# Attention tiles of batches 2, 4 and 6: matmuls in two 64-row halves of the array instead of four 64 x 64 quarters

## The chip, the cores and the metric

The kernel runs on one core of one Trainium2 chip. The metric is the device time of one execution in microseconds (us); of several runs the median is given. The profiled execution is one further run, with a span (first to last instruction) of its own and a time of its own.

## The reference

Linear attention without a softmax, normalised per head, is followed by an MLP mixer over tokens and channels. All data are float32.

```python
kv  = einsum('bhsd,bhse->bhde', k, v)        # 64 x 64 for each of 8 batches and 8 heads
out = einsum('bhsd,bhde->bhse', q, kv)       # 576 rows each: the part that the change touches
out = out / sqrt(mean(out*out, -1) + 1e-6) * g_norm
x   = out.transpose(0, 2, 1, 3).reshape(8, 576, 512)
h   = relu(x.transpose(0, 2, 1) @ w_tok1) @ w_tok2     # tokens: 576 -> 256 -> 576
u   = x + h.transpose(0, 2, 1)
y   = u + relu(u @ w_ch1) @ w_ch2                      # channels: 512 -> 1536 -> 512
```

## The kernel before

Batches are worked in four pairs (0 to 3). Each pair goes through attention, then token mixing; after the last pair the channel mixing follows, with two levels of a Strassen-like scheme (products `ps_a`, `ps_b`, `ps_d`, `ps_v`, `ps_w`, `ps_c`), and takes most of the time. While pair n is in token mixing, the attention of pair n+1 is woven into it. That order is written out by hand in lists of short names (`start`, `middle`, `steady`, `last`, L1391 to L1458) that `play` calls one after the other; `keep` holds each engine to this program order.

The names that matter here: `kv..` and `kr.` form k'v of a batch (`kv`, L399, and `kv_rem`, L417); `e..` copies it to `kvp[side]`, where the rows 0 to 63 hold the even head and the rows 64 to 127 the odd head of each of four head pairs (`hp`). `a0` to `a3` are `attend(c)` (L465): c = 0 and 1 are the first batch of the pair (side 0), c = 2 and 3 the second batch; each makes 256 rows of the attention output for all 8 heads. `a4` (`attend_rem`) makes the last 64 rows of both batches. `q..`, `g..` and `t..` read the result from PSUM (square on ScalarE; product with the gain and sum on VectorE). `h..` and `hr` are the first token product (`tok1`; `tok1_rem`, L621), `u0` to `u8` the second (`tok2`). Pair 0 uses other functions (`attend_tile`), so `attend` serves pairs 1, 2 and 3.

In TensorE's program order the tiles c = 0 and 1 stand so:

- pair 1: `hr`, **a0**, `u0 u1 u2`, **a1**, `kv10`
- pairs 2 and 3: `h00 h01`, **a0**, `h10 h11`, `hr`, **a1**, `kv10`

Each matmul of `attend` contracts over the 64 entries of a head: the stationary operand (`lhsT`) is a slice of q with 64 columns, which are rows of the output, and the moving operand (`rhs`) is a 64 x 64 block of `kvp`. The rows of the array follow from the head (h), the columns from the output's partitions (n), so four matmuls (n, h) stand in four quarters of the array. The two heads write to two PSUM tiles, `o[0]` and `o[1]`. There are 2 t x 4 hp x 2 n x 2 h = 32 matmuls in a call. In the profile each float32 matmul appears as two passes (two LDWEIGHTS and two MATMUL records), 64 for a call. `tok1_rem` also contracts over 64 rows, a batch in each half of the rows, with 128 stationary columns and 512 moving ones. All these matmuls go through the helper in L136 and have this line in the profile; they are told apart by their tiles and their array forms, written as rows*columns (64*64, 64*128, 128*128).

Of the kernel before, what the change touches and what calls it, by code (L numbers as in the profile page):

```python
# [20 lines left out]
def kernel(  # L21
# [33 lines left out]
    P = 128  # L55
# [5 lines left out]
    J, JJ, HF, Q = 4, 5, 64, 32  # L61
# [73 lines left out]
    def matmul(*a, **kw):  # L135
        keep(nc.tensor.matmul(*a, **kw))  # L136


    qT, q_rest = {}, {}
# [249 lines left out]
    def attention(pair, groups):  # L389
# [75 lines left out]
        def attend(c):  # L465
            n = "o" if c else "kv"
            o = [ps[n].tile([P, 2, HP, D], F32, name="ps_o", tag=n) for _ in range(2)]
            side = c // 2
            for t in range(2):
                for hp in range(HP):  # L470
                    for n in range(2):
                        for h in range(2):
                            r = ds(h * D, D)
                            matmul(o[h][ds(n * HF, HF), t, hp],
                                   lhsT=qT[2 * pair + side][r, hp, ds((2 * (c % 2) + t) * P + n * HF, HF)],
                                   rhs=kvp[side][r, hp, :D], start=True, stop=True)
            for h in range(2):
                bank[c, h] = o[h].rearrange("p t k d -> p (t k) d")
# [113 lines left out]
        for c in range(5):  # L592
            if whole:
                steps |= {f"a{c}{t}": do(attend_tile, c, t) if c < 4 else attend_tile_rem
                          for t in range(parts(c))}
            else:
                steps[f"a{c}"] = do(attend, c) if c < 4 else attend_rem
            for h in range(parts(c)):
                steps |= {f"{n}{c}{h}": do(f, c, h) for n, f in zip("gqt", (gain, square, total))}
            for t in range(1 if c == 4 else 2):  # L600
                steps |= {f"{n}{c}{t}": do(f, c, t) for n, f in zip("spd", (scale, scale_pool, scale_vector))}
# [957 lines left out]
```

## Time and profile before

| | |
|---|---|
| time, median of 3 runs | 768.65 us (768.58 to 768.66) |
| profiled execution | 768.43 us |
| its span | 766.6 us |
| PE (TensorE matmul) busy | 761.2 us, 99% of the span |
| PEld (weight load) busy | 613.0 us, 80% |
| VectorE, ScalarE, GpSimd busy | 644.5, 279.0, 110.8 us |
| granted TensorE clock | 1.000 |
| `ps_o` passes in quarters (64*64) | 768 (12 calls of `attend`), PE busy 13.8 us |

"PE busy" joins the spans of overlapping passes; what a pass costs in a dense stretch is read from the distance between the starts of two stretches in the timeline. A pass's own duration also holds its way through the array, which overlaps with the next ones. The last matmul ends 3.2 us before the span does.

### The profile page before, as it was taken

How to read it: one execution, taken by the hardware profiler on the slowest of the kernel's cores; microseconds unless marked ns; L12 is line 12 of the kernel's file. 1: busy time of each engine (PE TensorE's matmuls, PEld its weight loads, DVE VectorE, ACT ScalarE, POOL GpSimd, SP SyncE). 2: the span in 40 equal slices, each digit the busy share in tenths (PEclk: the TensorE clock that was granted, in tenths of full speed). 3: DMA queues.
4: the chain of work that ended last, by engine and by line, in shares of the span. 5: the costliest groups of instructions: out<-in, count | busy, mean ns of one | idle time of the engine just before them, and what ended most of it. 6: DMA issues, size and time to landing. Idle time of an engine off the chain costs nothing.

```text
span 766.6 us, 12767 instructions
## 1 busy us (share of the span) xinstructions
PE 761.2 (99%) x4694; PEld 613.0 (80%) x4694; DVE 644.5 (84%) x958; ACT 279.0 (36%) x563; POOL 110.8 (14%) x121
## 2 busy tenths in 40 slices
PE   9999999999999999999999999999999999999998
PEld 8655555446888888888888888888888888888887
DVE  3868896997757779899969889997898996798997
ACT  3656575773210232511234242123352223325211
POOL 0003030203410000002240002042000218000204
PEclk9999999999999999999999999999999999999999
DMA  9999999799799785589998578999649879845689
GB/s 353 325 331 375 318 380 329 252 319 350 252 289 321 288 283 170 175 270 216 216 231 246 157 214 227 261 187 264 202 145 293 166 225 205 209 147 152 153 203 121
DMA packets 138941, 188.28 MB, mean 246 GB/s; under 512 B 48896, under 2 KB 97536, under 8 KB 136832
## 3 DMA queue, kind: packets, MB, share of 16 engines
q1 hardware_dynamic: 103200, 168.72, 69.1%
q0 software_dynamic: 34848, 18.36, 16.0%
q8 instruction: 38, 0.62, 0.3%
q10 hardware_dynamic: 832, 0.39, 0.2%
q14 instruction: 23, 0.19, 0.1%
HBM read 138.28 MB, written 49.15 MB: 244 GB/s over the span
## 4 chain that ended last, share of the span: by engine, by line
PE 96%; DMA 2%; DVE 1%; SPq 0%; ACT 0%; issue 0%; DVEq 0%
PE ps_d L136 28%; PE ps_b L136 19%; PE ps_a L136 19%; PE ps_u L136 8%; PE ps_h L136 8%; PE ps_v L136 5%; PE ps_c L136 3%; PE ps_w L136 2%; PE ps_kv L136 2%; PE ps_o L136 2%; DMA raw<-in_moe_w_tok_dram 2%; DMA v_in<-in_v_dram 1%; PE ps_r L136 0%; DVE x L506 0%; DVE ms L534 0%; DVE w_tok L213 0%
## 5 line engine op out<-in xcount | busy, mean ns | idle before, releaser
L136 PE MATMUL ps_d<-ui,w 128*128 128x256 f32 x504 | 118.6, 379 | 0.0
L136 PEld LDWEIGHTS ps_d<-ui,w 128*128 128x128 f32 x504 | 95.8, 190 | 13.0
L133 ACT COPY ps_d<-ps_a 128x768 f32<-128x768 f32 (+1 forms) x56 | 32.0, 572 | 199.9 <-PE ps_a L136 196.9
L127 DVE TENSOR_TENSOR v<-v,v 128x1536 f32<-128x1536 f32 (+2 forms) x70 | 103.3, 1483 | 0.3
L136 PE MATMUL ps_b<-sv,w 128*128 128x256 f32 x324 | 78.9, 379 | 0.0
L136 PE MATMUL ps_a<-v,w 128*128 128x256 f32 x324 | 78.7, 379 | 0.0
L1288 POOL DMA_DIRECT2D out_dram<-us x24 | 26.8, 1836 | 291.8 <-ACT p L133 286.5
L136 PEld LDWEIGHTS ps_b<-sv,w 128*128 128x128 f32 x324 | 61.2, 190 | 8.9 <-issue 0.6
L136 PEld LDWEIGHTS ps_a<-v,w 128*128 128x128 f32 x324 | 61.6, 190 | 8.4
L136 PE MATMUL ps_u<-h,w_tok 128*128 128x512 f32 (+1 forms) x160 | 64.7, 599 | 0.0
L130 ACT ACTIVATE v<-v 128x768 f32<-128x768 f32 (+1 forms) x54 | 42.7, 822 | 55.1 <-DVE v L127 50.7
L136 PE MATMUL ps_d<-v,w 128*128 128x256 f32 x258 | 62.7, 379 | 0.0
L136 PE MATMUL ps_h<-x,w_tok 128*128 128x512 f32 x128 | 57.6, 600 | 0.7 <-DVE w_tok L213 0.6
L1288 POOL DMA_DIRECT2D out_dram<-r x40 | 41.3, 1926 | 102.0 <-ACT p L133 80.3
L136 PE MATMUL ps_d<-sv,w 128*128 128x256 f32 x228 | 55.4, 379 | 0.0
L136 PEld LDWEIGHTS ps_d<-v,w 128*128 128x128 f32 x258 | 49.0, 190 | 6.6
L136 PEld LDWEIGHTS ps_u<-h,w_tok 128*128 128x128 f32 (+1 forms) x160 | 25.6, 179 | 31.1 <-issue 27.0
L136 PEld LDWEIGHTS ps_d<-sv,w 128*128 128x128 f32 x228 | 43.3, 190 | 5.9
L136 PE MATMUL ps_a<-uT,w 128*128 128x256 f32 x192 | 46.7, 379 | 0.0
L136 PEld LDWEIGHTS ps_h<-x,w_tok 128*128 128x128 f32 x128 | 23.5, 190 | 28.3 <-issue 24.2
L136 PE MATMUL ps_b<-ui,w 128*128 128x256 f32 x168 | 40.8, 379 | 0.0
L136 PEld LDWEIGHTS ps_a<-uT,w 128*128 128x128 f32 x192 | 36.5, 190 | 5.0
(176 smaller groups left out, 1294.7 us busy)
## 6 DMA issues: line engine op xcount, KB each, us to landing
w<-parts SPq DMA_DIRECT2D x168, 384.0 KB
w<-parts SPq DMA_DIRECT2D x56, 192.0 KB
uT<-blocks SPq DMA_DIRECT2D x36, 256.0 KB
k_in<-in_k_dram SPq DMA_DIRECT2D x8, 1024.0 KB
v_in<-in_v_dram SPq DMA_DIRECT2D x8, 1024.0 KB
qT<-in_q_dram SPq DMA_DIRECT2D x8, 1024.0 KB
out_dram<-x POOLq DMA_DIRECT2D x16, 512.0 KB, 6.8
raw<-in_moe_w_ch_dram SPq DMA_DIRECT2D x8, 768.0 KB
```

The source lines that it names most:

```text
L127: keep(engine.tensor_tensor(out=o, in0=a, in1=b, op=op))
L130: keep(nc.scalar.activation(o, a, AF.Relu))
L133: keep(nc.scalar.copy(o, a))
L136: keep(nc.tensor.matmul(*a, **kw))
L1288: keep(nc.gpsimd.dma_start(to, t()[ds(b * Q, Q), at].rearrange("p n l j -> p n (l j)"), accum_op=ALU.add))
```

## The change

For c = 0 and 1 the two matmuls of a head pair and row block that differ only in their 64 columns become one with all 128 columns. The output partitions of this one matmul are 0 to 127; the array rows are still those of the head. A call then has 16 matmuls of the form 64*128 (32 passes) in place of 32 of the form 64*64. The tiles c = 2 and 3 and `attend_rem` stay in quarters. No other instruction on any engine changes place, operands or waits. Six calls are touched: a0 and a1 of pairs 1, 2 and 3.

```diff
             side = c // 2
+            wide = P if c < 2 else HF
             for t in range(2):
                 for hp in range(HP):
-                    for n in range(2):
+                    for n in range(P // wide):
                         for h in range(2):
                             r = ds(h * D, D)
-                            matmul(o[h][ds(n * HF, HF), t, hp],
-                                   lhsT=qT[2 * pair + side][r, hp, ds((2 * (c % 2) + t) * P + n * HF, HF)],
+                            matmul(o[h][ds(n * wide, wide), t, hp],
+                                   lhsT=qT[2 * pair + side][r, hp, ds((2 * (c % 2) + t) * P + n * wide, wide)],
                                    rhs=kvp[side][r, hp, :D], start=True, stop=True)
```

## The prediction

> **What bounds the kernel now.** I read the page first. Its engine line and its chain of work that ended last:
>
> ```profile
> PE 761.2 (99%) x4694; PEld 613.0 (80%) x4694; DVE 644.5 (84%) x958; ACT 279.0 (36%) x563; POOL 110.8 (14%) x121
> ...
> PE 96%; DMA 2%; DVE 1%; SPq 0%; ACT 0%; issue 0%; DVEq 0%
> ```
>
> TensorE works all the time and the chain runs through it. The reader should then ask whether it ever waits for anybody. The list of waits of PE, complete, answers:
>
> ```profile
> PE ps_j L136 <- DVE ones L1366: 1.1, 1, 1.1
> PE ps_h L136 <- DVE w_tok L213: 0.6, 1, 0.6
> PE ps_kv L136 <- DMA v_in<-in_v_dram: 0.4, 1, 0.4
> ```
>
> Three waits, and the last of them ends at 28.0 us (the `ps_h` one). From there to the end of its last matmul PE has no idle time; after that comes a tail of 3.2 us for the output. The first touched call starts at 44.4 us. So what a touched call takes more or less on TensorE moves everything behind it by the same amount: no wait lies behind it that could swallow a delay or eat up a gain. The question is only how long 16 matmuls in halves take against 32 in quarters. That is read from the timeline of PE (start, length, count); a stretch's cost is the distance to the next start:
>
> ```profile
> 110.12 0.46 PE L136 MATMUL ps_kv<-v_in,k_in 64*64 64x64 f32 x16
> 110.40 1.11 PE L136 MATMUL ps_o<-kvp,qT 64*64 64x64 f32 x64
> 111.44 7.13 PE L136 MATMUL ps_h<-x,w_tok 128*128 128x512 f32 x16
> 118.51 1.16 PE L136 MATMUL ps_o<-kvp,qT 64*64 64x64 f32 x64
> 119.60 7.13 PE L136 MATMUL ps_h<-x,w_tok 128*128 128x512 f32 x16
> 126.67 1.99 PE L136 MATMUL ps_h<-x,w_tok1r 64*128 64x512 f32 x8
> 128.58 1.16 PE L136 MATMUL ps_o<-kvp,qT 64*64 64x64 f32 x64
> 129.67 2.48 PE L136 MATMUL ps_kv<-v_in,k_in 128*64 128x64 f32 x80
> ```
>
> 118.51 is a0 and 128.58 is a1 of pair 3: 1.09 us each, for 64 passes, that is 16 rounds of four quarters. The six touched calls hold 6 x 1.09 = 6.5 us, 0.85% of the time. This is all that the change can touch.
>
> **What a round costs.** Each pass needs its stationary operand loaded. The groups of weight loads, forms kept apart (busy us, mean ns):
>
> ```profile
> L136 PEld LDWEIGHTS ps_o<-kvp,qT 64*64 64x64 f32 x768 | 12.3, 135 | 7.6 <-issue 5.3 <-PE ps_h L136 1.5 <-ACT h L130 0.8
> L136 PEld LDWEIGHTS ps_o<-kvp,qT 128*128 128x128 f32 x64 | 7.5, 192 | 0.6 <-issue 0.5
> L136 PEld LDWEIGHTS ps_h<-x,w_tok1r 64*128 64x128 f32 x32 | 2.8, 186 | 4.2 <-issue 4.2
> ```
>
> A load of 128 columns takes 51 to 57 ns longer than one of 64, whether it has 64 rows or 128: columns cost, rows don't. The change halves the number of loads and doubles the columns of each. How closely loads follow each other is seen in narrow windows of the weight loads' timeline: first the remainder product `ps_h<-x,w_tok1r`, the only work before that uses the array in the form that the change chooses, then the quarters of a1:
>
> ```profile
> 126.66 0.19 PEld L136 LDWEIGHTS ps_h<-x,w_tok1r 64*128 64x128 f32 x2 [0.76 <-issue]
> ...
> 126.77 0.19 PEld L136 LDWEIGHTS ps_h<-x,w_tok1r 64*128 64x128 f32 x2
> ...
> 128.58 0.15 PEld L136 LDWEIGHTS ps_o<-kvp,qT 64*64 64x64 f32 x4 [0.76 <-PE ps_h L136]
> ...
> 128.64 0.27 PEld L136 LDWEIGHTS ps_o<-kvp,qT 64*64 64x64 f32 x12
> ```
>
> In the halves two loads run together, one for each half (x2, both done in 0.19), and the next two start 0.11 us later. In the quarters four run together and the next four start 0.055 us later. So loads of different parts of the array overlap, and a part takes its next weights every 0.11 us with 128 columns, every 0.055 with 64.
>
> The moving operand stays 64 wide. A 512-wide pass takes 0.429 us (16 passes 7.07 us, and 32 passes 13.93 us elsewhere in the timeline; the difference by 16), so 64 columns take about 0.053. In quarters load and pass are even, and the round is (1.09 less 0.15 at the ends) / 16 = 0.058. In halves the load is twice as long as the pass and sets the round. The nearest dense row of 128-column loads is pair 0's extra tile:
>
> ```profile
> 14.19 1.06 PE L136 MATMUL ps_og<-kvg,qT 128*128 128x128 f32 x8
> 15.08 1.95 PE L136 MATMUL ps_o<-kvp,qT 128*128 128x128 f32 x16
> ```
>
> 8 passes in 0.89 us, 0.111 each. Its pass is as long as its load, so it bounds a round of halves from above, if the halves overlap; the bare distance of loads, 0.109, bounds it from below. I take 0.111, since it holds the hand-over from load to pass that the quarters show too (0.058 against 0.055).
>
> The Trainium skill, "TensorE: Matmul & The Clock Gate", section "LDWEIGHTS (loading the stationary operand)", says that a load takes its columns divided by 1.2 in ns, whatever its rows, 107 ns for 128: a rule that speaks against this change. By it alone the sum below would be 4.0 us instead of 4.5; the trace's 0.109 to 0.111 is a little above, and I use the trace.
>
> **The ends of a stretch.** 16 passes of 128x512 take 7.07 us where 16 x 0.429 is 6.86: 0.21 us goes at the ends when the array form changes. One part is the load with nothing beside it, 0.11 (the quarters' call 110.40, which follows quarters, takes 1.04 and not 1.09: 0.05, one 64-column load). The rest, 0.10, is the emptying of the array: `ps_kv` at 110.12, with quarters behind it, goes over to them without it (0.28 us for four rounds of 0.058 and a load), while 1.09 - 16 x 0.058 - 0.055 leaves 0.10 for calls with another form behind. The wait of PE for itself shown at 128.58 is this: the record of the pass before it ends later than that start, so no wait for a result is in it.
>
> **The sum.** A call in halves between other forms: 16 rounds x 0.111 = 1.78, plus a first load of 0.11, plus emptying 0.10, less 0.058 since behind the last pass no load is awaited: 1.93 us, 0.84 more than 1.09. This holds for a1 of pair 1 and a0 of pairs 2 and 3: 3 x 0.84 = 2.52.
>
> The other three (a0 of pair 1, a1 of pairs 2 and 3) stand right behind `hr`, which has the form 64*128 already. For them the change takes away one change of form: 0.09 of emptying behind `hr` (0.52 from its last pass to the next start, of which the pass is 0.43), and the first load goes under `hr`'s last pass, 0.11. Its operands are there: `kvp` is copied for a0 of pair 1 by 43.0 us, over 0.8 us before. So 0.84 - 0.20 = 0.64 each, 3 x 0.64 = 1.92. On their other side, and between all other stretches, the changes of form stay as they are.
>
> Sum: +4.5 us. On the profiled execution's 768.43 that makes 772.9; the median of the runs stands 0.22 above it, so 768.65 + 4.5 = 773.1, slower by 0.58%.
>
> Everything else I cost at nothing. ScalarE and VectorE read the same PSUM tiles with the same instructions, 0.6 to 0.8 us later; next to use these banks are `kv10` or the next pair of calls, which stand behind on TensorE and move with it. DMA loads get 4.5 us more, and PE waits for none of them. If this cover failed, the eviction of one tile (0.68 us) would show as a wait of `ps_kv`; I see no reason.
>
> Bounds: the round 0.109 to 0.115 (the upper is an estimate: the hand-over of 0.003 that the quarters show, doubled and rounded up), times 16 x 6: -0.2 to +0.4. The gain behind `hr` 0 to 0.6. Together +4.3 to +5.5, or 773.0 to 774.2. The low end goes to 772.4, since distances are read to 0.01 us and several make up a call, some 0.1 a call. The far rows, 0.058 and 0.22 a round, are the rivals that follow.
>
> **Rivals.**
>
> *The moving operand still sets the round.* If a half took its 128 columns as two sets of 64 side by side, as the quarters do, a round would stay 0.058: 16 of them as now, and only the gain behind `hr` is left, 3 x (0.09 + 0.05) = 0.4 us. Time 768.2, no change. It decides if loads follow at less than 0.06. For it: the quarters do fill the whole array in 0.055. Against it: the 0.11 between loads in the very same form. Chance 0.06.
>
> *Passes bound by their number.* The quarters start a pass every 0.94 / 64 = 0.015 us. If that were the limit, 32 passes would take 0.48: 6 x 0.46 = 2.8 us less, with the gain behind `hr` 3.2, 765.4. Against it: `ps_kv` in two column halves (129.67, 80 passes in 2.41) starts one every 0.030, so the limit is per part of the array, not per instruction; and 16 passes of 0.053 in one half can't be done in 0.48. Chance 0.02. The same skill page, in "Wait — 56ns, not 53.3ns?", gives a floor of about 25 ns from start to start however small the matmul; by it the quarters would take 1.6 and the halves 0.8 us a call, 4.8 us saved. The trace disagrees with 15 ns.
>
> *Halves don't overlap when loads are dense.* In `hr` a load has 0.43 us of pass to hide under; in the new calls it has 0.053. If the two halves took turns, a round would be 0.22: 16 x 0.11 x 6 = 10.5 us on top, 783.6. If a load only couldn't run under its own half's pass, 0.165 a round, 778.3. Against: quarters load and pass at the same rate without either. Chance 0.03 for both.
>
> *It isn't what it says:* the instructions listed for the changed kernel are 128x64, 16 in a call, in six calls, with the same waits, so 0.01.
>
> **How the numbers follow.** The forecast has 0.88. A difference within 0.2% (1.5 us) is about what a measurement of this kernel can't tell from none; the first rival lies there, with most of the last: 0.07. Faster: 0.02. Slower: 0.91. The forecast's own range, 772.4 to 774.2, holds the 8 in 10 and needs no other case.
>
> **What would show it.** In the profile after: 192 `ps_o` passes of form 64*128, 64x64 moving, with 384 left in quarters; the distance from such a call to the next start 1.93 us between other forms and about 1.83 behind `hr`, with `hr` itself 1.83 instead of 1.92; loads of one half every 0.11 us; no new wait of PE; the start of the channel stage (`ps_v`, 182.38 now) 4.5 us later, and nothing added after it. A distance near 1.09 would mean the first rival, 0.5 the second, 2.7 or 3.6 the third. A shift that shrinks after 187 us would mean that the chain has slack I didn't see.

## The result, and the profile after

The changed kernel takes 772.61 us, median of 4 runs (772.35 to 772.69), against 768.65 us for the kernel before beside it (768.58 to 768.84): 3.96 us more by the medians. The ratio of the runs is 1.0046, with a 95% interval from 1.0033 to 1.0060. On 768.65 us the ratio makes 772.2 us, the interval 771.2 to 773.3. The forecast was +4.5 us, 773.1. The median lies within the range that was stated (772.4 to 774.2), in its lowest eighth; the time by the ratio lies 0.2 below it.

The page of the changed kernel, its engine line and its chain:

```profile
PE 765.0 (99%) x4502; PEld 618.8 (80%) x4502; DVE 645.0 (84%) x958; ACT 279.7 (36%) x563; POOL 110.8 (14%) x121
...
PE 96%; DMA 2%; DVE 1%; SPq 0%; ACT 0%; issue 0%; DVEq 0%
```

192 passes fewer, and TensorE is busy 3.8 us longer. The list of waits of PE, complete:

```profile
PE ps_j L136 <- DVE ones L1367: 1.1, 1, 1.1
PE ps_kv L136 <- DMA v_in<-in_v_dram: 0.7, 1, 0.7
PE ps_h L136 <- DVE w_tok L213: 0.6, 1, 0.6
```

All three lie in the start, as before; the change brings no new wait. The timeline of PE around pair 3's touched calls (start, length, count; the price is the distance to the next start):

```profile
112.66 0.46 PE L136 MATMUL ps_kv<-v_in,k_in 64*64 64x64 f32 x16
112.94 1.11 PE L136 MATMUL ps_o<-kvp,qT 64*64 64x64 f32 x64
113.99 7.13 PE L136 MATMUL ps_h<-x,w_tok 128*128 128x512 f32 x16
121.05 2.00 PE L136 MATMUL ps_o<-kvp,qT 64*128 64x64 f32 x32
122.98 7.13 PE L136 MATMUL ps_h<-x,w_tok 128*128 128x512 f32 x16
130.05 1.99 PE L136 MATMUL ps_h<-x,w_tok1r 64*128 64x512 f32 x8
131.87 1.90 PE L136 MATMUL ps_o<-kvp,qT 64*128 64x64 f32 x32
133.69 2.48 PE L136 MATMUL ps_kv<-v_in,k_in 128*64 128x64 f32 x80
```

a0 between other forms takes 1.93 us, a1 behind the remainder product 1.82, and the remainder product itself 1.82 (130.05 to 131.87) where it took 1.91. The untouched a3 at 112.94 takes 1.05, as before. The weight loads show why. First their group (busy us, mean ns; the quarters' loads still take 135 ns), then the first loads of a0 in narrow windows:

```profile
L136 PEld LDWEIGHTS ps_o<-kvp,qT 64*128 64x128 f32 x192 | 11.4, 188 | 3.7 <-issue 2.5 <-ACT x L570 0.8 <-PE ps_h L136 0.5
```

```profile
121.05 0.19 PEld L136 LDWEIGHTS ps_o<-kvp,qT 64*128 64x128 f32 x2 [0.76 <-ACT x L570]
...
121.16 0.19 PEld L136 LDWEIGHTS ps_o<-kvp,qT 64*128 64x128 f32 x2
```

Two loads together, one for each half, and the next two 0.11 us later. From there the rounds go on at that pace: single passes of the trace start 0.111 us apart (121.212, 121.323, 121.434, 121.546), each 0.055 us behind the start of its load.

The whole shift is made before the channel stage. Call by call, from the starts in the two traces: +0.735, +0.734 and +0.736 us behind the remainder product, +0.839, +0.841 and +0.839 elsewhere, and three times -0.096 in the remainder product. The sum is 4.724 - 0.288 = 4.44 us. From the end of the attention to the last matmul the two kernels stay apart by 4.01 to 4.02 us.

### The profile page after: what moved, and what is told of

Same layout as the page of the kernel before. It is cut to its first block, busy times and chain, and to the rows that moved or that the text cites. A ratio compares the mean times of both kernels' runs of the same rounds, so it can differ in the third digit from the quotient of the medians.

```text
span 770.5 us, 12383 instructions
## 1 busy us (share of the span) xinstructions
PE 765.0 (99%) x4502; PEld 618.8 (80%) x4502; DVE 645.0 (84%) x958; ACT 279.7 (36%) x563; POOL 110.8 (14%) x121
## 4 chain that ended last, share of the span: by engine, by line
PE 96%; DMA 2%; DVE 1%; SPq 0%; ACT 0%; issue 0%; DVEq 0%
PE ps_d L136 28%; PE ps_b L136 19%; PE ps_a L136 19%; PE ps_u L136 8%; PE ps_h L136 8%; PE ps_v L136 5%; PE ps_c L136 3%; PE ps_o L136 2%; PE ps_w L136 2%; PE ps_kv L136 2%; DMA raw<-in_moe_w_tok_dram 1%; DMA v_in<-in_k_dram 1%; PE ps_r L136 0%; DVE x L507 0%; DVE ms L535 0%; DVE w_tok L213 0%
```

## The experiments

Theory A: in a dense stretch a part of the array takes a new round every max(load, pass); the load goes by the columns of the stationary operand (0.055 us for 64, 0.111 for 128), the pass by those of the moving one (0.053 for 64, 0.107 for 128). Rivals: load and pass of a half follow one another, or the number of passes counts. A second question came from the profile after: why 3.9 to 4.0 and not 4.4.

**The changed kernel once more** (e1), no edit.

> The changed kernel once more, timed in five rounds, for its distance to the kernel before and for a second profile of it. By the distances between stretches in the two profiles at hand (calls +0.735 and +0.84 us, the remainder product in front of three of them -0.096), the change itself is worth 3 x 0.84 + 3 x 0.735 - 3 x 0.096 = +4.4 us; the two profiles differ by only 3.9, because the profile of the changed kernel had 0.32 us less in pair 0's ps_kv stretch near 19 us and 0.16 less in pair 1's ps_r stretch near 59 us. Theory A: both are accidents of one execution; here the touched calls repeat to 0.01 us, the two stretches may come out either way, and the median lies 4.0 to 4.5 above the kernel before. Theory B: the changed calls shorten both stretches for good; then both are short again here and the median lies 3.9 above.

772.37 us (5 runs) against 768.53 us; ratio 1.0049 (1.0036 to 1.0062). In the trace every touched call repeats to 0.002 us, and both stretches are short again: ps_r 0.577, ps_kv near 19 us 2.61. The distance of medians, 3.84, is lower than theory A (accidents alone) allows; for ps_r that speaks for a lasting effect of the change, and it is followed up below.

**The moving operand doubled, in halves and in quarters** (e2 and e3; e3 differs from e2 in `wide = HF`).

```diff
-                            matmul(o[h][ds(n * wide, wide), t, hp],
+                            at = t * HP + hp
+                            m = 2 * D if c < 2 and at < 2 * HP - 1 else D
+                            matmul(o[h].rearrange("p t k d -> p (t k d)")[ds(n * wide, wide), ds(at * D, m)],
...
-                                   rhs=kvp[side][r, hp, :D], start=True, stop=True)
+                                   rhs=kvp[side][r, hp, :m], start=True, stop=True)
```

> The changed kernel, with a moving operand of 128 columns instead of 64 in the touched calls (the upper 64 land in the place of the next head pair, which is overwritten by the next matmul; the last matmul of a call stays 64 wide). Theory A: in halves the load of 128 columns (0.109 to 0.111 us) sets the round and a pass of 64 columns (0.053) hides under it; a pass of 128 (0.107) still hides, so a call stays at 1.93 and 1.83 us and the time at 772.6 us, within 0.5. Rival: load and pass of a half follow each other, 0.055 + 0.053, and the round only happens to be 0.11; then 0.053 x 16 x 6 = 5.1 us more, 777.7.

> The kernel before (quarters, loads of 64 columns), with the moving operand doubled to 128 columns in the same six calls as in the halves. Theory A: a round takes the longer of load (0.055) and pass (0.107), so it goes from 0.058 to about 0.111, a call from 1.09 to about 1.84 us, +4.5 us in all, 773.1: about what the halves cost. Rival (a round is bound by the number of passes, or by load plus pass): no change, 768.7, or a round of 0.165 and +10 us, 779.

Halves with 128 moving columns: 772.60 us, ratio 1.0050 (1.0037 to 1.0063), the same as the changed kernel. Quarters with 128: 772.62, ratio 1.0053 (1.0040 to 1.0066). a0 of pair 3 and the stretch behind it, first in e2, then in e3:

```profile
121.18 2.00 PE L136 MATMUL ps_o<-kvp,qT 64*128 64x128 f32 x32
123.11 7.13 PE L136 MATMUL ps_h<-x,w_tok 128*128 128x512 f32 x16
```

```profile
121.14 1.87 PE L136 MATMUL ps_o<-kvp,qT 64*64 64x128 f32 x64
122.94 7.13 PE L136 MATMUL ps_h<-x,w_tok 128*128 128x512 f32 x16
```

In halves twice the streamed columns cost nothing: 1.93 us as with 64. In quarters the same doubling takes a call from 1.09 to 1.80. So a pass of up to 107 ns hides under the load of 128 columns, and a load of 64 under such a pass. Theory A holds, and it also gives the size: by single starts a round of 64-column loads with 128 moving columns takes 0.109 us, nearly as much as the 0.111 of 128-column loads with 64. The calls differ more, 1.80 against 1.93 us, at their ends. The rival of load plus pass (777.7 and 779) and the one of the number of passes (768.7 for e3) are out.

**One tile at a time** (e6 and e7), `wide = P if c < 1 else HF`, and `wide = P if c == 1 else HF`.

> Halves for the tile c = 0 alone (a0 of pairs 1, 2, 3), a1 in quarters as before. By the distances measured so far: pair 1's a0 +0.735 less 0.096 in the remainder product in front of it, pairs 2 and 3 +0.84 each, less the 0.16 of ps_r: +2.15 us, 770.7. Rival (a call costs the same wherever it stands, 4.4 / 6 each): +2.2, and a1 behind the remainder product unchanged at 1.09; told apart by the calls in the trace: 1.83 behind the remainder product, 1.93 elsewhere.

> Halves for the tile c = 1 alone. Pair 1's a1 +0.84, pairs 2 and 3 +0.735 less 0.096 each, less 0.16 of ps_r: +1.95 us, 770.5. With c = 0 alone the two add up to the whole change, 2.15 + 1.95 = 4.1, plus the 0.16 that both take away: 4.25. If the calls helped or hindered each other, the sum would differ.

c = 0 alone: 770.31 us, ratio 1.0022 (1.0013 to 1.0032); c = 1 alone: 770.14, ratio 1.0017 (1.0007 to 1.0027), beside 768.53. In the traces the touched calls cost what they cost in the whole change, to 0.002 us: 0.736, 0.840, 0.840, and -0.097 in pair 1's remainder product; 0.839, 0.735, 0.737, and -0.096 and -0.098. So the distances add up: 2.32 + 2.12 = 4.44. Both timings come out below the expectation, by 0.39 and 0.36 us. They are 0.54 and 0.51 below the sum of the calls, and the whole change is 0.48 below its own: about the same whichever tile is touched, so it is no part of the price of the calls. The rival with one price for every place is out: 1.83 behind the remainder product, 1.93 elsewhere, and where a1 stays in quarters it takes 1.09 behind it.

**All four tiles in halves** (e8), `wide = P`.

> Halves for all four tiles of a pair. a2 loses its neighbour of the same form (ps_r stays in quarters): +0.84 and 0.11 + 0.05 for the change of form, 1.0 in each of three pairs; a3 of pairs 1 and 2 follows kr1's like in quarters, 1.0 each; a3 of pair 3 stands between other forms, 0.84. Together +5.8 on top of the changed kernel, 778.3. Rival (neighbours don't matter, 4.4 for six calls): +4.4, 777.0.

778.75 us, ratio 1.0124 (1.0109 to 1.0139), 6.1 above the changed kernel's 772.61. a2 of pair 3 and its neighbours:

```profile
145.74 2.00 PE L136 MATMUL ps_o<-kvp,qT 64*128 64x64 f32 x32
147.67 0.69 PE L136 MATMUL ps_r<-kvp,qR 64*64 64x64 f32 x32
148.30 8.85 PE L136 MATMUL ps_u<-h,w_tok 128*128 128x512 f32 x20
```

a2 now takes 1.93 us instead of 0.98, which was cheap because ps_r follows in the same form, and ps_r 0.63 instead of 0.58: 1.0 together, as expected. a3 behind kr0 goes from 1.04 to 1.93, and kr0 from 0.28 to 0.39. Summed over the pairs the trace gives 5.84, expected were 5.8. The neighbours count.

**Quarters, put next to each other** (e4), a trial at a faster kernel.

```diff
-"-a3 -q30 ..." ... "a0 q00 g01 q01 g00"            (pairs 2 and 3)
+"-a3 a0 -q30 ..." ... "q00 g01 q01 g00"
-"a1 q10 g11 q11 g10 ...", "kv10 kv11 kr1 e10 ..."    (pairs 1, 2 and 3)
+"kv10 kv11 kr1 a1 q10 g11 q11 g10 ...", "e10 ..."
```

> Quarters as in the kernel before, but stretches of the same array form put next to each other: a0 of pairs 2 and 3 right behind a3 of the pair before (both in quarters), a1 of pairs 1, 2 and 3 right behind kr1 (in quarters too). From the rows of the kernel before a stretch between other forms loses 0.155 us in quarters and 0.21 in 128 x 512 at its ends. Two a0 moved: 2 x (0.155 + 0.21) = 0.73; three a1 moved: 3 x 0.15 = 0.45. Theory A: 1.2 us less, 767.5. Rival: a0 comes so early that it waits for the copies of kvp, or the later eviction of a1 holds up ps_kv or ps_u; then 0.5 us less or nothing, with a wait of PE or a longer stretch behind the moved calls.

772.54 us, ratio 1.0051 (1.0038 to 1.0065): 4 us slower, not 1.2 faster. The moved a1 does take 1.04 and kr1 0.28, as expected. But the waits of PE have three new entries, and the timeline of pair 3 shows the longest:

```profile
PE ps_o L136 <- issue: 2.1, 1, 2.1
PE ps_o L136 <- ACT kvp L133: 1.3, 1, 1.3
...
PE ps_r L136 <- issue: 0.7, 1, 0.7
```

```profile
112.22 1.81 PE L136 MATMUL ps_o<-kvp,qT 64*64 64x64 f32 x111
116.14 0.50 PE L136 MATMUL ps_o<-kvp,qT 64*64 64x64 f32 x17 [2.12 <-issue]
116.57 1.98 PE L136 MATMUL ps_h<-x,w_tok 128*128 128x512 f32 x4
```

One is the rival of the expectation (a0 waits for the copies of kvp). The two others end with no releaser ("issue"): TensorE stops in the middle of a call, after 111 of 128 quarter passes, 47 of them a0's own. By then a0 has read every block of `kvp` once and has written to both of its PSUM tiles, so neither explains the stop.

The 1.2 us of theory A are there, and more than eaten up. From the start of pair 1's remainder product to the channel stage the trace takes 143.66 us, the kernel before 139.93: 3.73 more. Three stretches are 4.92 longer: pair 1's ps_r by 0.82, and the double calls a3 a0 by 1.72 in pair 2 (the copies of kvp) and 2.38 in pair 3, against 1.98 for such a call without a stop (e10 below). The remaining -1.19 is what the neighbours save.

**The kernel before once more, and what stops ps_r** (e5, no edit; e9 and e10).

> The kernel before once more, for a second profile. Theory A1: the 0.16 us in pair 1's ps_r stretch (0.741 us there, 0.576 in the three profiles with longer calls) belongs to the kernel before and repeats, and the 0.3 us in pair 0's ps_kv stretch near 19 us is an accident of the first profile, here 2.6 to 2.9. Theory B1: both are accidents; then ps_r takes 0.576 here.

ps_r of pair 1 in the first profile of the kernel before, in this second one, and in the changed kernel:

```profile
58.92 0.81 PE L136 MATMUL ps_r<-kvp,qR 64*64 64x64 f32 x32
59.66 1.12 PE L136 MATMUL ps_u<-h,w_tok 128*128 128x512 f32 x2
```

```profile
58.80 1.01 PE L136 MATMUL ps_r<-kvp,qR 64*64 64x64 f32 x32
59.74 1.13 PE L136 MATMUL ps_u<-h,w_tok 128*128 128x512 f32 x2
```

```profile
60.14 0.65 PE L136 MATMUL ps_r<-kvp,qR 64*64 64x64 f32 x32
60.72 1.56 PE L136 MATMUL ps_u<-h,w_tok 128*128 128x512 f32 x3
```

0.74 and 0.94 us against 0.58: the kernel before loses 0.17 us here in its first profile and 0.36 in its second, and the changed kernel nothing in either. So the halt repeats, as theory A1 has it. ps_kv near 19 us takes 2.67 here, so the 2.91 of the first profile was an accident. Where does the halt come from? Counting TensorE's weight loads, matmuls and sequencer entries in order of their start, the halt comes behind the 1473rd in both profiles of the kernel before, and behind the 1473rd and the 3009th in e4. Divided by 256, all leave 193.

```diff
-        "j21 zk00 zk01 ka00 ...
+        "j5 zk00 zk01 ka00 ...
```

> The kernel before with 5 instead of 21 of the warming matmuls ahead of all work: 32 passes (64 instructions of TensorE) fewer, nothing else; the start may get slower by a microsecond. In two profiles of the kernel before, pair 1's ps_r stretch halts near TensorE's instruction 1473, and in the reordered kernel it halts near 1472 and again, for 2.3 us, near 3009: both leave 193 when divided by 256, and the instruction queue's packets are of 16 KB, 256 instructions of 64 bytes if a packet holds that many. Theory S (TensorE runs out of fetched instructions in a dense stretch of small matmuls): with 64 instructions fewer in front, the halt falls 32 passes later, among 512-wide passes where it costs nothing, and ps_r takes 0.576 us. Rival (ps_r waits for data or a buffer): it still takes 0.74 to 0.94.

> The reordered quarters with 5 warming matmuls. Theory S: the halts of 0.8 us in pair 1's ps_r and of 2.3 us in pair 3's a0 behind a3 go (stretches 0.58 and about 1.98 for the two calls), the wait of pair 2's a0 for the copies of kvp (about 1.5 us) stays. Rival: all three stay.

With 64 instructions fewer in front, ps_r takes 0.577 us in both (e9's time, 769.08 in one run, holds a start 0.9 us later at the first touched call). In e10 the 2.1 us halt of pair 3 is gone too: the double call takes 1.98 us where it took 4.35. And a new halt stands elsewhere, in pair 1's a1:

```profile
56.43 0.99 PE L136 MATMUL ps_o<-kvp,qT 64*64 64x64 f32 x54
57.57 0.44 PE L136 MATMUL ps_o<-kvp,qT 64*64 64x64 f32 x10 [0.16 <-issue]
```

It comes behind the 1217th instruction, and 1217 leaves 193 again. Five halts in three kernels at one place of a 256-instruction block, moving with the count and not with the data.

The packet records show that TensorE runs out of instructions. The DMA queue that the profile's page lists as "q8 instruction" moves one 16 KB packet for each 256 of TensorE's entries, 38 for the 9701 of the kernel before and 36 for the 9317 of the changed one; here the packets are matched to the blocks by their order. In each of the five halts TensorE goes on 1.34 to 1.48 us after the end of the packet that brings the block. At the other 450 block boundaries counted in the 13 traces that packet had ended 1.57 us or more before, and there is no halt. In e3 and e11 the boundary lies in pair 1's ps_r as well, but 1.96 and 1.98 us behind its packet, and ps_r takes 0.576 us.

e10's time, 771.27 us in one run, holds a start 3.3 us later at pair 1's remainder product; from there to the channel stage it takes 139.54 us, 0.4 less than the kernel before. Pair 2's wait for kvp, expected to stay, shrank as well (the double call took 2.47 instead of 3.70 us); that was not followed further. e9 alone would prove little, for ps_r also went through without a halt in e11, whose order is the old one up to there: in this order the halt is a close race, 0 to 0.36 us.

**Only a1 moved, in pairs 2 and 3** (e11).

> Quarters as before; of the reordering only a1 of pairs 2 and 3 right behind kr1. In the reordered kernel these two places ran without a halt. Theory A: one change of form fewer in each, 2 x 0.155 = 0.3 us less, 768.2 against 768.5, too little for the timing to tell from no change but plain in the trace (1.04 and 1.05 us instead of 1.09 for a1, 0.28 instead of 0.39 for kr1). Rival: the later eviction of a1 holds up what follows, or a halt falls into the denser stretch; 768.6 to 771.

768.33 us against 768.61; ratio 0.9996 (0.9987 to 1.0005), so no difference that can be told. The trace has the gain at its place, 1.04 us for both moved a1 and 0.28 for kr1. As a whole it gains nothing: the traced execution (769.55 us) is the slowest of the 11, and in pairs 2 and 3 PE waits three times where the kernel before doesn't, 0.5 us for a DMA of `qT` and twice 0.2 for ScalarE. Whether the move brings these waits is open.

## Where the prediction was right, and the step that failed

**The bound.** Right for the touched calls: PE carries the chain before and after, no new wait came, and what the calls lost reached the end.

**The round.** Right, and shown by e2 and e3: 0.111 us, set by the load of 128 columns; calls of 1.93 and 1.83 us were expected, 1.93 and 1.82 to 1.83 measured. The estimate by the Trainium skill alone ("TensorE: Matmul & The Clock Gate", section "LDWEIGHTS (loading the stationary operand)"), 4.0 us, would have been 0.4 too low for the calls.

**The ends of a stretch.** Right: 0.096 taken out of the remainder product (0.09 expected), and 0.104 saved in the call behind it (0.839 less 0.735; 0.11 expected). e8 shows the same terms with the opposite sign.

**The sum.** Its two parts, 2.52 and 1.92, make 4.44, which the prediction writes as 4.5. Measured call by call it is 4.44.

**The step that failed** is "Everything else I cost at nothing", together with "no wait lies behind it that could swallow a delay or eat up a gain". The kernel before had a halt of its own behind the touched calls, in pair 1's ps_r, 0.17 and 0.36 us in its two profiles, and the changed kernel has none. With 128 instructions fewer in front, its block boundary comes at 67.0 us, behind ps_r and over 6 us after its packet. Fewer instructions are not the only way out: e3 has as many as the kernel before, and its longer calls gave the packet time enough. The list of PE's waits could not show the halt: a pass is 0.22 us long or more in the records, so the joined spans of the passes had a gap of at most 0.05 us. Distances of starts show it, 741 ns for ps_r in pair 1 against 577 in pair 2.

That leaves 4.1 to 4.3 of the 4.44. The rest of the way lies in the two ends of the program, where executions differ by that much: pair 1's remainder product starts at 42.45 and 42.33 us in the two profiles of the kernel before, at 42.20 in both of the changed one, and at 42.19 to 42.40 in e2, e3, e6 and e7; the tail behind the last matmul takes 3.2 and 3.5 us before, 3.1 after. For the first profile of each kernel the terms add up: 4.44 less 0.17 (halt), 0.25 (start) and 0.11 (tail) is 3.91 us, and the two executions differ by 3.92. That the medians (3.96, and 3.84 in e1) divide in the same way is not shown. Why both profiles of the changed kernel have an early start is open; no instruction that the change touches runs before 44 us.

**The range.** Its low end allowed 0.6 us for reading errors in the calls and nothing for these terms. The calls came out as summed, so that the median still lies inside is luck: an allowance made for something else covered it, and the time by the ratio, 772.2, falls below it even so. A range from 771.9 up would have covered the halt and the ends.

**The rivals.** "The moving operand still sets the round" is out by the 0.111 us and by e2; "passes bound by their number" by e3, where as many passes take 1.80 us; "halves don't overlap" by a call of 1.93 us.

## What to carry to other kernels

Before merging small matmuls into fewer, write down for one part of the array the load (columns of the stationary operand) and the pass (columns of the moving one): here the longer was the price of a round, so a merge that doubles the stationary columns costs least where the load stays under the pass. Even with load and pass about equal (128 moving columns) halves took 1.93 us and quarters 1.80; wider passes were not tried. Count the changes of array form as well: each cost about 0.10 us plus the first load here, and neighbours of the same form save it, unless the denser stretch brings a halt or a wait. And look for small halts in the distances of starts, not only in the list of waits.

## What the runs showed that I had not expected

Dense quarter passes can outrun TensorE's supply of instructions. 128 quarter passes are 256 instructions and take 1.9 us; halts that cost 0.17 to 2.4 us came in such stretches, all five at the same position modulo 256 and each until 1.34 to 1.48 us after its packet. Why some packets come late was not followed further. In the first profile of each of the two kernels the instruction queue's 16 KB packets took 0.9 to 1.5 us each during the attention, when the DMA engines were mostly busy. The Trainium skill, "Runtime: NRT & Kernel Launch", section "Instruction fetch mechanics", says that instructions are fetched in blocks of 16 KiB, 256 of them, and that crossing a block is mostly hidden. The block size agrees with the positions; hidden it is not in e4, where the longest halt shows 2.1 us of idle time. So the fewest instructions are not the fastest here, but the kernel with the most of them in a row pays too: halts, and the wait for `kvp`, took from the reordered quarters more than their neighbours saved.
